# A fast block product for the last of eight projections, with its sums filled into idle time

## The chip, the cores and the metric

One NeuronCore of a Trainium2 chip runs the whole program. The metric is the device time of one execution in microseconds (us); the profiled execution is one such run taken by the hardware profiler. Engines are TensorE (PE; PEld is its weight load), VectorE (DVE), ScalarE (ACT), GpSimd (POOL) and SyncE (SP, which issues the DMAs).

## The reference

Attention with two fixed masks over 8 batches, 8 heads and 576 positions, and on its output x a gated feed-forward block:

```python
h = np.maximum(x @ w_in, 0.0)          # x: (8, 576, 512), w_in: (512, 1024)
u, v = (h[..., :d_ff // 2], h[..., d_ff // 2:])
v_n = (v - mu) / np.sqrt(var + 1e-06)  # over the last axis of v
v_s = np.einsum('ts,bsd->btd', w_spatial, v_n) + b_spatial[None, :, None]
gated = u * v_s
return (gated @ w_out).astype(np.float32)
```

The change touches u = max(x @ w_in[:, :512], 0) of batch 7 alone, and the multiply u * v_s of that batch.

## The kernel before

All products are done in fp32 precision out of two reduced-precision parts: a number is stored as a rounded part and a rest ("hi" and "lo"), and each product is three matmuls (`PROD`). So each operand of a product needs a cast (`rnd`, L492, on ACT, DVE or POOL) and a subtraction, the rest (`rest`, L506, on DVE or POOL).

The eight batches run one after the other. For each there are, in this order, the attention (scores, softmax, output x), V (`project_v`, L1092, matmuls L1072 with 512 columns), the normalisation of V (statistics L1027, a reciprocal root on POOL at L1040, the normalising step L1047), the out-projection of the batch before (`project_out`, L1446, matmuls L1465), U (`project_u`, L1111, matmuls L1132 of 128x288) and the gate, which multiplies V by `w_spatial` (`gate`, L1396, matmuls L1415) and then by U. The rows beyond position 512 are the "tail", 64 rows with their own operands (`tail`, `tail_b`) and their own matmuls (L1205, L1206).

In `project_u` each of 8 blocks of the result (two halves of positions, four row blocks) sums over 4 contraction blocks of 3 matmuls each, 96 in all, and an ACT instruction evicts it from PSUM with the ReLU (L1146).

For batches 6 and 7 (`FAST_S`) the gate is `gate_fast` (L1287), a seven-product scheme for a product of 2x2 blocks: it forms sums of the blocks of V (`total`, by `combine`, L918) and of `w_spatial`, multiplies seven pairs (`product`, matmuls L1331, phases 0 to 6 by name: a11, a12, s2, s1, s4, s3, a22), and adds the results up. Two pairs of PSUM banks, x and z, take the phases in turn: 0 into x, 1 into z, 2 onto x, 3 into z anew, 4 onto z, 5 and 6 onto x. A result that is needed twice is copied out (`keep`, L522), and a bank is added to a copy by DVE (`join`, L1363) before it is written anew. The last products are multiplied by U at L1216 (`times`).

The order of the work is not written by hand. Each operation is added with a due time (its key, from the table `KEYS`), the engines that may run it and a price for each. `Program.order` (L202) plays this forward with a list scheduler: whichever engine is free next takes the ready operation with the smallest key, unless another engine would end it earlier. The model lets DVE and POOL instructions marked with `port` exclude each other. `settle` (L364) then tries a few rearrangements of matmuls, and `emit` (L415) writes every engine's instructions in that order.

The row names below have the buffer numbers taken off: `x`, `v_raw`, `vn`, `k`, `q`, `pp` are buffers that serve several purposes over time, `m` is a PSUM bank, `g` the gated product on its way into the out-projection, `o` a copy out of PSUM, `bn` the statistics.

Of the kernel before, what the change touches and what calls it, by code (L numbers as in the profile page):

```python
# [21 lines left out]
HF = DFF // 2  # L22
# [40 lines left out]
    "tt": (6.0,),  # L63
    "tp": (-10.0, 40.0,),
# [6 lines left out]
FETCHED, FETCH_COST = 100.0, 32.0  # L71
STEP_IN, STEP_OUT = 93.0, 108.0
# [8 lines left out]
FAST_S = (6, 7)  # L81
U_IN_X = tuple(b + 1 for b in U_FIRST)
# [78 lines left out]
class Program:  # L161
# [3 lines left out]
    def __init__(self):  # L165
        self.ops, self.writer, self.readers, self.spare = [], {}, {}, {}
        self.tiled, self.port, self.kind, self.lead, self.took = {}, {}, {}, {}, {}

    def add(self, key, choices, fn, reads=(), writes=(), spare=None, tiled=0, port=(), kind=0, lead=None, took=None):
# [32 lines left out]
    def order(self):  # L202
# [22 lines left out]

        def release(n):
            for e, _ in ops[n][1]:
                heapq.heappush(wait[e], (ready_at[n][e], n))
# [7 lines left out]
        for n in range(len(ops)):  # L236
            if not left[n]:
                release(n)
        while len(issued) < len(ops):
# [75 lines left out]
    def timed(self, rows):  # L315
# [5 lines left out]
        opens = {}  # L321

        def opened(e):
# [4 lines left out]
            if any(d not in done for d in self.ops[n][3]):  # L328
                return None
            start = max([free[e], *(done[d] + LAT[on[d]][e] for d in self.ops[n][3])])  # L330
            return start, n

        while len(done) < len(self.ops):
# [28 lines left out]
        return max(*free.values(), streamed + DMA_TAIL), at  # L362

    def settle(self, issued):  # L364
# [3 lines left out]
        best, at = self.timed(rows)  # L368
        moved = True
        while moved:  # L370
# [10 lines left out]
            for (a, b), (c, d) in zip(runs, runs[1:]):  # L381
# [4 lines left out]
                for new in (  # L386
# [3 lines left out]
                    if got and got[0] < best - JOIN_GAIN:  # L390
                        best, at = got
# [46 lines left out]
def attention_moe(ctx, tc, qT, kT, ks, vl, vs, cst, w_in, w_out, wsp, wtail, out):  # L438
# [36 lines left out]
    r_vn = Ring(sb, "vn", [P, 2, NT, HF], F32R, 1)  # L475
# [482 lines left out]
    def weights():  # L958
# [3 lines left out]
        first = r_vn.new()  # L962
        for n, (key, name, i, c) in enumerate(jobs):

            def put(key=key, name=name, i=i, c=c, n=n):
                stage = (first, n) if n < NT else ((r_g if n % 2 else r_u).new(), 0)
# [120 lines left out]
    vns, tls, us, xtl, split_last = {}, {}, {}, {}, {}  # L1087
# [692 lines left out]
```

## Time and profile before

| | |
|---|---|
| median of 3 runs | 506.44 us (506.10 to 506.92) |
| profiled execution | 506.58 us, of which 504.8 us are its span |
| PE busy | 491.0 us (97% of the span) |
| DVE busy | 365.6 us (72%) |
| ACT busy | 290.3 us (58%) |
| POOL busy | 113.7 us (23%) |
| mean granted TensorE clock | 0.99 |
| chain that ended last | PE 93%, DMA 3%, DVE, POOL and ACT 1% each |

The times in the trace count from the start of the span. The part that matters lies at its end: U of batch 6 to 427.3, the gate of batch 6 from 427.3 to 442.0, V of batch 7 to 451.8, the out-projection of batch 6 to 462.9, U of batch 7 to 475.7, and the gate of batch 7 with the last out-projection to 504.8.

### The profile page before, as it was taken

Reading aid. Unit: us, or ns where it says so; the run is one execution under the profiler, and the core shown is the slowest. Engines: PE = TensorE matmul, PEld = TensorE weight load, DVE = VectorE, ACT = ScalarE, POOL = GpSimd, SP = SyncE. Lnnn points to the kernel's source line nnn. Section 1 sums busy time; section 2 is a strip of 40 time slices with the busy share of each in tenths; the row PEclk is TensorE's granted clock in tenths of the full one; section 3 lists DMA queues with packets and bytes.
Section 4 is the critical chain, followed back from the end, with each engine's and each line's share of the span. In section 5 each row is a group of like instructions: output and inputs, shape, how many; then the busy total and the mean of one; then the engine's idle time right before and its main releaser. Section 6 shows DMA issues by size and latency. Waiting matters only on the chain.

```text
span 504.8 us, 15798 instructions
## 1 busy us (share of the span) xinstructions
PE 491.0 (97%) x6374; PEld 451.3 (89%) x6374; DVE 365.6 (72%) x1114; ACT 290.3 (58%) x896; POOL 113.7 (23%) x232
## 2 busy tenths in 40 slices
PE   6599999999999999999999999999999999999997
PEld 3478898889988999899998999989999899989996
DVE  4889898987778628785389834778269796959285
ACT  5797777677546566373554764355464465435334
POOL 4554325133232013120121211121022302011000
PEclk9699999999999999999999999999999999999999
DMA  8997342432423502205224152023321051002002
GB/s 288 404 342 239 125 155 93 137 93 53 156 90 120 175 5 91 77 25 165 82 93 139 45 163 89 5 90 119 86 92 47 0 190 47 2 1 94 1 1 94
DMA packets 26968, 54.47 MB, mean 108 GB/s; under 512 B 3216, under 2 KB 11536, under 8 KB 26896
## 3 DMA queue, kind: packets, MB, share of 16 engines
q1 hardware_dynamic: 26896, 53.47, 32.0%
q8 instruction: 50, 0.82, 0.7%
q14 instruction: 22, 0.18, 0.1%
HBM read 44.02 MB, written 9.44 MB: 106 GB/s over the span
## 4 chain that ended last, share of the span: by engine, by line
PE 93%; DMA 3%; DVE 1%; POOL 1%; ACT 1%; issue 0%; SPq 0%; POOLq 0%
PE m L1132 21%; PE m L1072 20%; PE m L1465 18%; PE m L1415 15%; PE m L1331 4%; PE po L705 4%; PE po L809 3%; PE s L595 3%; PE s L738 2%; DMA q<-qT 1%; PE m L1427 1%; PE m L1428 1%; DMA k<-kT 1%; PE m L1206 0%; POOL ptl L502 0%; PE m L1205 0%
## 5 line engine op out<-in xcount | busy, mean ns | idle before, releaser
L1132 PE MATMUL m<-x,w_in_sb 128*128 128x288 f32 x768 | 105.2, 297 | 0.0
L1132 PEld LDWEIGHTS m<-x,w_in_sb 128*128 128x128 f32 x768 | 103.0, 188 | 0.6
L1072 PE MATMUL m<-w_in_sb,x 128*128 128x512 f32 (+1 forms) x408 | 99.6, 398 | 0.0
L1465 PE MATMUL m<-g,w_out 128*128 128x288 f32 x672 | 93.4, 296 | 0.2
L1465 PEld LDWEIGHTS m<-g,w_out 128*128 128x128 f32 x672 | 90.1, 188 | 2.0 <-ACT o L522 0.3
L1072 PEld LDWEIGHTS m<-w_in_sb,x 128*128 128x128 f32 (+1 forms) x408 | 74.1, 185 | 18.3
L1415 PE MATMUL m<-wsp_sb,vn 128*128 128x288 f32 x576 | 85.0, 296 | 0.0
L1415 PEld LDWEIGHTS m<-wsp_sb,vn 128*128 128x128 f32 x576 | 79.2, 189 | 0.7
L502 POOL TENSOR_SCALAR ptl<-pc 32x64 f32<-32x64 f32 (+3 forms) x98 | 38.2, 389 | 108.6 <-DVE pc L676 70.5
L652 ACT ACTIVATE pl<-pl,ml 128x64 f32<-128x64 f32 (+1 forms) x140 | 47.0, 338 | 7.8 <-DVE ml L632 7.6
L1040 POOL TENSOR_TENSOR bn<-bn,sel 128x1 f32<-128x1 f32 (+1 forms) x37 | 21.6, 586 | 131.3 <-DVE bn L1035 126.5
L510 DVE TENSOR_TENSOR g<-u,g 128x288 fp32r<-128x288 f32 x98 | 43.8, 464 | 8.6 <-POOL g L502 4.1
L500 ACT CAST g<-u 128x288 fp32r<-128x288 f32 x89 | 38.1, 435 | 19.7 <-DVE u L921 9.5
L500 ACT COPY ptl<-pc 32x320 f32<-32x320 f32 (+3 forms) x94 | 33.5, 356 | 17.2 <-DVE pc L676 15.3
L1146 ACT ACTIVATE u<-m 128x288 f32<-128x288 f32 x56 | 23.0, 410 | 35.5 <-PE m L1132 35.2
L1027 DVE BATCH_NORM_STATS2 bn<-vv 128x6 f32<-128x512 f32 (+1 forms) x29 | 19.8, 685 | 29.3 <-ACT vv L1022 29.0
L510 DVE TENSOR_TENSOR x<-po,x 128x288 fp32r<-128x288 f32 x64 | 27.4, 448 | 9.3 <-DMA v_raw<-vl 4.7
L1022 ACT ACTIVATE vv<-m 128x512 f32<-128x512 f32 (+1 forms) x29 | 17.2, 595 | 28.7 <-PE m L1072 28.4
L522 ACT CAST x<-po 128x288 fp32r<-128x288 f32 x60 | 22.2, 399 | 18.7 <-PE po L705 9.8
L632 DVE CUSTOM_DVE_ANT_0 pl<-s,cst_sb 128x64 f32<-128x64 f32 (+1 forms) x140 | 22.1, 214 | 13.0 <-PE s L595 13.0
L652 ACT ACTIVATION_READ_ACCUMULATOR pl<-pl,ml 128x1 f32 (+1 forms) x140 | 26.4, 189 | 0.0
L502 POOL TENSOR_SCALAR pts<-pc 32x288 f32<-32x288 f32 x30 | 15.7, 523 | 40.6 <-DVE pc L792 31.5
(182 smaller groups left out, 738.7 us busy)
## 6 DMA issues: line engine op xcount, KB each, us to landing
q<-qT SPq DMA_DIRECT2D x32, 295.0 KB, 4.2
v_raw<-vs SPq DMA_DIRECT2D x15, 512.0 KB, 4.1
v_raw<-vl SPq DMA_DIRECT2D x16, 384.0 KB, 4.1
k<-kT SPq DMA_DIRECT2D x16, 304.0 KB, 4.8
kbd<-ks SPq DMA_DIRECT2D x32, 144.0 KB, 5.0
outT<-o SPq DMA_DIRECT2D x32, 144.0 KB, 1.9
outT<-u SPq DMA_DIRECT2D x28, 144.0 KB, 2.1
vn<-w_in SPq DMA_DIRECT2D x4, 512.0 KB, 7.6
```

Of the source, the lines that this page charges most:

```text
L500: eng.copy(dst(), src())
L502: eng.tensor_scalar(dst(), src(), 1.0, 0.0, op0=ALU.mult, op1=ALU.add)
L510: eng.tensor_tensor(dst(), src(), f32(hi()), op=ALU.subtract)
L522: eng.copy(dst(), src())
L632: eng.tensor_tensor_reduce(out=p_sb()[:m, u, :], in0=s_ps[u % 2]()[:m, f0 : f0 + 2 * STRIDE], in1=msk[:m], scale=-SCALE, scalar=3.0e38, op ...
L652: eng.activation(p_sb()[:m, u, :], src, AF.Exp, bias=st()[:m, u : u + 1], scale=SCALE if masked else -1.0, **total,)
L1040: lambda eng: eng.tensor_tensor(bn()[:m, 9:10], bn()[:m, 8:9], sel[:m, 0:1], op=ALU.pow),
L1072: eng.matmul(v_ps()[:m, :], x_at(kt)[:, a, :], w_in_sb[:, w, kt, HF:], start=(n == 0 and i == 0), stop=(n == NT - 1 and i == 2),)
L1132: eng.matmul(u_ps()[:, :HS], w_in_sb[:, w, kt, f * P : (f + 1) * P], xs[NHP * b + kt]()[:, a, r], start=(n == 0 and i == 0), stop=(n == NT ...
L1146: lambda eng, u=u, f=f, u_ps=u_ps: eng.activation(flat(u)[:, f * HS : (f + 1) * HS], u_ps()[:, :HS], AF.Relu),
L1415: eng.matmul(s_ps()[:, :HS], vn()[:, a, kt, fs], wsp_sb[:, w, kt, r], start=(kt == 0 and i == 0), stop=False,)
L1465: eng.matmul(o_ps()[:, :HS], w_out_t[0]()[:, w, r, BLOCKS[name], j * P : (j + 1) * P], at(a), start=(first and r == 0 and i == 0), stop=(r ...
```

## The change

`project_u` hands batch 7 to a new `project_u_fast` (`FAST_U`). It is the same seven-product scheme with x as the moving and `w_in` as the stationary operand: 7 products of 2 row blocks, 2 contraction blocks and 3 matmuls, 84 in all. It needs four sums of blocks of x (`t1` to `t4`) and four of `w_in` (`s1` to `s4`), each with a cast and a rest; `one_row` adds them for each of two contraction blocks. Results are copied out by ACT without the ReLU, six joins are done by DVE, and the ReLU moves into the multiplies of batch 7's gate, which become `scalar_tensor_tensor` instructions.

The sums are added while `prog.quiet` is set. Such operations are left out when `order` plays the program forward, so the rest is ordered without them; `fill_idle` then takes them one by one and tries up to 12 gaps (`IDLE_TRIES`) of DVE or POOL that are at least 0.9 of the price long (`FIT`), keeping the place after which the modelled end is earliest.

To make room, the buffer of the normalised V is split in two (`vn0`, `vn1`), and operands of `gate_fast` that stood in x buffers move: phases 2 and 3 to `vn1`, phase 4 to `xt`. This holds for batches 6 and 7, so the gate of batch 6 is ordered anew too.

```diff
+FIT, IDLE_BIAS, IDLE_TRIES, IDLE_EPS = 0.9, 300.0, 12, 15.0
+FAST_U = (7,)
...
+        if self.quiet:
+            self.idle.append(n)
...
+    def fill_idle(self, issued):
...
+        best, at, done = self.timed(rows)
+        for n in self.idle:
+            found = []
+            for e, cost in self.ops[n][1]:
+                ready = max([done[d] + LAT[on[d]][e] for d in self.ops[n][3]], default=0.0)
+                row = rows[e]
+                for i in range(len(row) + 1):
+                    begins = at[row[i]] if i < len(row) else 1e12
+                    if begins < ready:
+                        continue
+                    since = max(ready, done[row[i - 1]] if i else 0.0)
+                    if begins - since >= FIT * cost:
+                        found.append((since + cost + (IDLE_BIAS if e == POOL else 0.0), e, i))
+            tried = []
+            for _, e, i in sorted(found)[:IDLE_TRIES]:
+                new = {**rows, e: rows[e][:i] + [n] + rows[e][i:]}
+                got = self.timed(new)
+                if got:
+                    tried.append((got[0], e, i, new, got))
+                    if got[0] <= best + IDLE_EPS:
+                        break
+            _, e, _, rows, (best, at, done) = min(tried, key=lambda x: x[0])
+            on[n] = e
...
-        issued = self.settle(issued)
+        issued = self.settle(self.fill_idle(issued))
...
-    r_vn = Ring(sb, "vn", [P, 2, NT, HF], F32R, 1)
+    r_vn = [Ring(sb, f"vn{i}_", [P, NT, HF], F32R, 1) for i in range(2)]
...
+    def project_u_fast(b, key):
...
+        prog.quiet = False
+        x, z = ([r_pm.new(held) for _ in range(2)] for _ in range(2))
...
+        product(0, "a11", "11", x)
+        keep(0, x, 0, 0)
+        product(1, "a12", "21", z)
+        join(1, z, 0, 0)
+        product(2, "s2", "t2", x, False)
+        keep(2, x, 0, 1)
+        product(3, "s1", "t1", z)
+        keep(3, z, 1, 1)
+        product(4, "s4", "22", z, False)
+        join(4, z, 0, 1)
+        product(5, "s3", "t3", x, False)
+        join(5, x, 1, 1)
+        product(6, "a22", "t4", x, False)
+        keep(6, x, 1, 0)
+
+    def one_row(key, n, r, row, rtok, values, sums, out, kept, after, engs):
...
+        cost = lambda n: [(e, {DVE: 70 + 1.04 * n, POOL: 120 + 2.3 * n}[e]) for e in engs]
+        for j in range(2):
+            hi, lo, toks = values(j)
+            add(
+                key, cost(2 * n),
+                lambda eng, j=j, hi=hi, lo=lo: eng.tensor_tensor(
+                    row[j]()[:, : 2 * n], f32(hi()), f32(lo()), op=ALU.add
+                ),
+                [*toks, *after], [rtok(j, 0), rtok(j, 1)], port=(DVE, POOL), kind=1,
+            )
+        for x, y, d, op in sums:
...
+        for name, where in out:
+            at, tok = kept[name]
+            rnd(key, n, lambda at=at: at(0, r), part(*where), [rtok(*where)], [tok(r)[0]], (ACT,))
+            rest(
+                key, n, lambda at=at: at(1, r), part(*where), lambda at=at: at(0, r),
+                [rtok(*where), tok(r)[0]], [tok(r)[1]], engs,
+            )
...
+                if b in FAST_U:
+                    add(
+                        k0 - KEYS["so"][2], [(DVE, 70 + 1.04 * HS)],
+                        lambda eng, o=o, ug=ug: eng.scalar_tensor_tensor(
+                            ug(), ug(), 0.0, o(), op0=ALU.max, op1=ALU.mult
+                        ),
+                        [(o,)], [utok], port=(DVE,),
+                    )
+                    continue
```

How the instructions stand on an engine before and after is listed below at three places around the gate of batch 6. A row is the line, the operation, output and inputs, and the shape; x2, x3 or x6 is a run of like rows. In the names, `m` is a PSUM bank, `v_raw`, `x`, `xt` and `vn__7` hold operands of the products, `kbd`, `ptl` and `pc` parts of `w_spatial` sums, `tail` and `tail_b` the operands of the tail.

PE at the start of the gate of batch 6, before, from the second product on; `kbd` with `x` is the third product, `kbd` with `v_raw` a part of the sixth, and the last two rows are the fourth:

```order
L1331 MATMUL m_6674<-wsp_sb,v_raw_6465 128x288 x6
L1331 MATMUL m_6684<-wsp_sb,v_raw_6465 128x288 x3
L1205 MATMUL m_6674<-wt_h,tail_6645 128x288
L1206 MATMUL m_6674<-wt_b,tail_b_73 128x288
L1331 MATMUL m_6684<-wsp_sb,v_raw_6465 128x288 x3
L1205 MATMUL m_6684<-wt_h,tail_6645 128x288
L1206 MATMUL m_6684<-wt_b,tail_b_73 128x288
L1331 MATMUL m_6650<-kbd_6498,x_6638 128x288 x6
L1331 MATMUL m_6662<-kbd_6498,x_6638 128x288 x6
L1331 MATMUL m_6650<-kbd_6498,v_raw_6678 128x288 x6
L1331 MATMUL m_6674<-wsp_sb,x_6643 128x288 x6
L1331 MATMUL m_6684<-wsp_sb,x_6643 128x288 x6
```

PE there after; the first two rows are the first product; L1542 is the former L1331, and L1267 and L1268 are the tail's:

```order
L1542 MATMUL m_6677<-wsp_sb,v_raw_6409 128x288 x6
L1542 MATMUL m_6689<-wsp_sb,v_raw_6409 128x288 x6
L1542 MATMUL m_6702<-wsp_sb,v_raw_6478 128x288 x6
L1542 MATMUL m_6714<-wsp_sb,v_raw_6478 128x288 x6
L1267 MATMUL m_6702<-wt_h,tail_6687 128x288
L1268 MATMUL m_6702<-wt_b,tail_b_73 128x288
L1267 MATMUL m_6714<-wt_h,tail_6687 128x288
L1268 MATMUL m_6714<-wt_b,tail_b_73 128x288
L1542 MATMUL m_6677<-kbd_6534,vn__7_6429 128x288 x6
L1542 MATMUL m_6689<-kbd_6534,vn__7_6429 128x288 x6
L1542 MATMUL m_6702<-wsp_sb,vn__7_6429 128x288 x6
L1542 MATMUL m_6714<-wsp_sb,vn__7_6429 128x288 x6
```

The six matmuls of `kbd` with `v_raw`, which stood ahead of the fourth product, now stand behind it, and the tail's matmuls follow all of the first two products.

DVE from the tail's statistics to the two joins that free the banks of the fourth product, before:

```order
L1031 BN_AGGR bn_6618<-bn_6618 128x2
L1035 TENSOR_SCALAR bn_6618<-bn_6618 128x1
L1047 TENSOR_SCALAR vv_6608<-vv_6608,bn_6618 128x512
L510 TENSOR_TENSOR x_6638<-vn_6157,x_6638 128x512
L510 TENSOR_TENSOR tail_6645<-vv_6608,tail_6645 64x512
L510 TENSOR_TENSOR tail_6655<-vv_6608,tail_6655 64x512
L510 TENSOR_TENSOR x_6643<-vv_6404,x_6643 128x512
L510 TENSOR_TENSOR x_6666<-vn_6157,x_6666 128x512
L510 TENSOR_TENSOR v_raw_6678<-vn_6157,v_raw_6678 128x512
L510 TENSOR_TENSOR v_raw_6701<-vn_6157,v_raw_6701 128x512
L1363 TENSOR_TENSOR o_6672<-m_6674,o_6672 128x288
L1363 TENSOR_TENSOR o_6688<-m_6684,o_6688 128x288
```

DVE there after (L569 is the rest, L980 a combination, L1574 the join, L1482 and L1490 the new sums):

```order
L1345 TENSOR_TENSOR pc_79<-k_6593,pc_79 96x288
L1094 TENSOR_SCALAR bn_6641<-bn_6641 128x1
L1482 TENSOR_TENSOR k_6666<-x_6311 128x576
L1106 TENSOR_SCALAR vv_6630<-vv_6630,bn_6641 128x512
L1490 TENSOR_TENSOR k_6615<-k_6666,k_6615 128x288
L569 TENSOR_TENSOR tail_6687<-vv_6630,tail_6687 64x512
L569 TENSOR_TENSOR tail_6698<-vv_6630,tail_6698 64x512
L569 TENSOR_TENSOR v_raw_6712<-vn__7_6164,v_raw_6712 128x512
L1574 TENSOR_TENSOR o_6693<-m_6702,o_6693 128x288
L569 TENSOR_TENSOR v_raw_6725<-vn__7_6164,v_raw_6725 128x512
L980 TENSOR_TENSOR u_6505<-o_6693,u_6505 128x288
L1574 TENSOR_TENSOR o_6706<-m_6714,o_6706 128x288
```

Two new sums (`k_6666`, `k_6615`) stand among the steps of the tail, and a rest and a combination now stand between the two joins.

POOL from the last cast ahead of the gate, before:

```order
L502 TENSOR_SCALAR g_1668<-u_5639 128x288
L1040 TENSOR_TENSOR bn_6618<-bn_6618,sel 128x1
L502 TENSOR_SCALAR x_6643<-vv_6404 128x512
L502 TENSOR_SCALAR tail_b_73<-vv_6608 64x512
L502 TENSOR_SCALAR tail_b_74<-vv_6608 64x512
L1040 TENSOR_TENSOR bn_6841<-bn_6841,sel 128x1
```

POOL there after:

```order
L561 TENSOR_SCALAR xt_6643<-vn__7_6164 128x512
L1099 TENSOR_TENSOR bn_6641<-bn_6641,sel 128x1
L561 TENSOR_SCALAR tail_6687<-vv_6630 64x512
L561 TENSOR_SCALAR tail_6698<-vv_6630 64x512
L1490 TENSOR_TENSOR k_6666<-k_6666,k_6615 128x288
L561 TENSOR_SCALAR tail_b_74<-vv_6630 64x512
L569 TENSOR_TENSOR x_6664<-k_6615,x_6664 128x288
L1490 TENSOR_TENSOR k_6666<-k_6666 128x288
L569 TENSOR_TENSOR x_6802<-k_6666,x_6802 128x288
```

The casts of `tail` are on POOL now, and four new sums and rests (L1490, L569) follow among and behind the casts; five more rows like these come next. Over the whole program POOL gets 15 instructions of two wide inputs, 10 of L1490, one of L1482 (512 columns) and four of L569.

## Rows read from the trace of the kernel before

**Rows 1.** The page, part 1: busy us, share of the span, instructions of each engine.

```profile
PE 491.0 (97%) x6374; PEld 451.3 (89%) x6374; DVE 365.6 (72%) x1114; ACT 290.3 (58%) x896; POOL 113.7 (23%) x232
```

**Rows 2.** The page, part 4: share of the chain that ended last, by engine.

```profile
PE 93%; DMA 3%; DVE 1%; POOL 1%; ACT 1%; issue 0%; SPq 0%; POOLq 0%
```

**Rows 3.** Windows: stretch, us, busy us (instructions) of PE, PEld, DVE, ACT, POOL; clock; DMA.

```profile
427.30:442.00 14.70, 14.70 (x108) 14.44 (x107) 13.67 (x30) 6.87 (x16) 2.04 (x3) 1.00 0.01 2
...
462.90:475.70 12.80, 12.80 (x99) 12.80 (x98) 3.78 (x7) 4.59 (x11) 0.55 (x1) 1.00 0.10 36
```

**Rows 4.** The chain in order of time: start us, us, engine, work, instructions.

```profile
442.17 9.79 PE m L1072 x42
...
463.06 12.80 PE m L1132 x96
```

**Rows 5.** DVE timeline 437 to 443: start us, us, engine, line, operation, out<-in, count.

```profile
439.40 0.82 DVE L921 TENSOR_TENSOR u<-u,u 128x288 f32<-128x288 f32 x2
440.14 0.45 DVE L1363 TENSOR_TENSOR o<-m,o 128x288 f32<-128x288 f32 x1
```

**Rows 6.** POOL by line and form: count, then busy us, mean ns, idle before.

```profile
L502 POOL TENSOR_SCALAR g<-x 128x288 fp32r<-128x288 f32 x3 | 1.3, 432 | 1.4 <-ACT pl L652 1.0 <-PE m L1465 0.4
...
L502 POOL TENSOR_SCALAR v_raw<-vn 128x512 fp32r<-128x512 f32 x2 | 1.2, 620 | 2.7 <-PE m L1331 1.8 <-PE m L1465 0.8
```

**Rows 7.** POOL timeline 424 to 437; in brackets idle before and what ended it.

```profile
425.73 0.55 POOL L1040 TENSOR_TENSOR bn<-bn,sel 128x1 f32<-128x1 f32 x1 [22.23 <-DVE bn L1035]
426.77 0.62 POOL L502 TENSOR_SCALAR x<-vv 128x512 fp32r<-128x512 f32 x1 [0.49 <-PE m L1132]
427.35 2.06 POOL L502 TENSOR_SCALAR tail_b<-vv 64x512 fp32r<-64x512 f32 x2
```

**Rows 8.** DVE timeline 424 to 437.

```profile
424.55 0.70 DVE L1027 BATCH_NORM_STATS2 bn<-vv 128x6 f32<-128x512 f32 x1 [1.95 <-ACT vv L1022]
...
426.32 0.55 DVE L1047 TENSOR_SCALAR vv<-vv,bn 128x512 f32<-128x512 f32 x1 [0.67 <-POOL bn L1040]
426.97 0.95 DVE L510 TENSOR_TENSOR x<-vn,x 128x512 fp32r<-128x512 f32 x1
427.96 2.00 DVE L510 TENSOR_TENSOR tail<-vv,tail 64x512 fp32r<-64x512 f32 x2
429.99 0.69 DVE L510 TENSOR_TENSOR x<-vv,x 128x512 fp32r<-128x512 f32 x1
...
431.20 1.29 DVE L510 TENSOR_TENSOR v_raw<-vn,v_raw 128x512 fp32r<-128x512 f32 x2
432.41 0.82 DVE L1363 TENSOR_TENSOR o<-m,o 128x288 f32<-128x288 f32 x2
...
435.58 0.46 DVE L1363 TENSOR_TENSOR o<-m,o 128x288 f32<-128x288 f32 x1 [0.66 <-PE m L1206]
```

**Rows 9.** DVE and POOL timelines 453.5 to 457.

```profile
453.67 0.17 DVE L1031 BATCH_NORM_AGGREGATE bn<-bn 128x2 f32<-128x6 f32 x1
453.78 0.46 DVE L921 TENSOR_TENSOR u<-u 128x288 f32<-128x288 f32 x1
...
455.02 0.45 DVE L510 TENSOR_TENSOR g<-u,g 128x288 fp32r<-128x288 f32 x1
...
454.82 0.69 POOL L1040 TENSOR_TENSOR bn<-bn,sel 128x1 f32<-128x1 f32 x1 [2.94 <-DVE bn L1035]
```

**Rows 10.** PE timeline 395 to 505, three rows of the gate of batch 6.

```profile
427.32 2.95 PE L1331 MATMUL m<-wsp_sb,v_raw 128*128 128x288 f32 x21
...
433.43 1.76 PE L1331 MATMUL m<-wsp_sb,x 128*128 128x288 f32 x12
...
440.95 0.94 PE L1331 MATMUL m<-ptl,v_raw 128*128 128x288 f32 x6
```

**Rows 11.** Waits of PE weight loads: what for, total us, times, longest us.

```profile
PEld m L1465 <- ACT o L522: 0.3, 1, 0.3
PEld m L1465 <- ACT u L522: 0.3, 1, 0.3
```

More of the change, by code (lines that the diff above doesn't have):

```diff
@@ L224, in begin @@
             return at
+        idle = set(self.idle)
         def release(n):
+            if n in idle:
+                for m in after[n]:
+                    for o in ENGINES:
+                        ready_at[m][o] = max(ready_at[m][o], ready_at[n][o])
+                    left[m] -= 1
+                    if not left[m]:
+                        release(m)
+                return
             for e, _ in ops[n][1]:
@@ L234, in queue @@
             )
[L236 to L239, printed above, removed]
+        for n in [n for n in range(len(ops)) if not left[n]]:
+            release(n)
+        while len(issued) < len(ops) - len(idle):
             best = None
@@ L321, in timed @@
         opens = {}
+        deps, total = self.needs(on), len(on)
         def opened(e):
@@ L327, in opened @@
             n = rows[e][heads[e]]
-            if any(d not in done for d in self.ops[n][3]):
+            if any(d not in done for d in deps[n]):
                 return None
-            start = max([free[e], *(done[d] + LAT[on[d]][e] for d in self.ops[n][3])])
+            start = max([free[e], *(done[d] + LAT[on[d]][e] for d in deps[n])])
             return start, n
-        while len(done) < len(self.ops):
+        while len(done) < total:
             best = None
@@ L361, in timed, with needs @@
             opens = {o: x for o, x in opens.items() if o != e and x}
-        return max(*free.values(), streamed + DMA_TAIL), at
+        return max(*free.values(), streamed + DMA_TAIL), at, done
+    def needs(self, on):
+        missing = set(self.idle) - set(on)
+        if not missing:
+            return {n: self.ops[n][3] for n in on}
+        found = {}
+        for n in range(len(self.ops)):
+            found[n] = set()
+            for d in self.ops[n][3]:
+                found[n] |= found[d] if d in missing else {d}
+        return {n: found[n] for n in on}
+    def fill_idle(self, issued):
+        on = {n: e for _, n, e in issued}
+        rows = {e: [n for _, n, o in issued if o == e] for e in ENGINES}
+        if not self.idle:
+            return issued
+        best, at, done = self.timed(rows)
[21 more added lines that the diff above has]
+            on[n] = e
+        return sorted((at[n], n, on[n]) for n in on)
     def settle(self, issued):
@@ L961, in weights @@
         )
-        first = r_vn.new()
+        first = [r.new() for r in r_vn]
         for n, (key, name, i, c) in enumerate(jobs):
             def put(key=key, name=name, i=i, c=c, n=n):
-                stage = (first, n) if n < NT else ((r_g if n % 2 else r_u).new(), 0)
+                stage = (first[n // 2], n % 2) if n < NT else ((r_g if n % 2 else r_u).new(), 0)
                 val, tok = in_value(c, i)
@@ L1285, in spatial_sums, with homes, home @@
         w_t["d"] = (wt_d, at_d)
+    def homes():
+        low = []
+        def home(phase):
+            if phase in (2, 3):
+                low.extend(r_vn[1].new() for _ in range(not low))
+                buf, view = low[0], lambda ap: ap[:, 2 * (phase - 2) : 2 * (phase - 1)].rearrange("p a b -> p (a b)")
+            elif phase == 4:
+                buf, view = r_xt.new(), lambda ap: ap.rearrange("p a b c -> p (a b c)")
+            else:
+                buf, view = r_v.new(), lambda ap: ap.bitcast(F32R).rearrange("p a b -> p (a b)")
+            at = lambda w: view(buf()).rearrange("p (a b c) -> p a b c", a=2, b=2)[:, w]
+            return at, lambda w: (buf, phase, w)
+        return home
```

142 lines of the change are left out of this document (117 added, 25 removed).

## The prediction, made before the changed kernel ran

> **What bounds the kernel now.** I began with the page's first part, where TensorE (PE) is busy 97% of the span [rows 1], and its fourth, where PE holds 93% of the chain that ended last [rows 2]. So a matmul less is time less, as long as PE never has to wait for what makes its operands. The windows by stage say where that condition is tight. The gate of batch 6 (427.3 to 442.0) is full on PE, and VectorE (DVE) is busy 13.67 of its 14.70 us; in U of batch 7 (462.9 to 475.7) DVE is busy 3.78 us and ScalarE (ACT) 4.59 of 12.80 [rows 3]. The granted clock is 1.00 in both, the upper of its two levels, so the clock has nothing to give or take while PE stays fed. The change takes matmuls from the second of these stages and puts its new sums mostly ahead of and into the first.
>
> **What it removes.** U of batch 7 is 96 matmuls of 128x288. As seven products, of 2 row blocks, 2 contraction blocks and 3 partial products each, it is 84. The chain gives 12.80 us for the 96, and 9.79 us for 42 of 512 columns [rows 4], thus 0.1333 and 0.2331 us for one. The twelve are worth 12 x 0.1333 = 1.60 us, and they lie on the path.
>
> **What it adds in that stage.** The eight ReLU evictions on ACT become eight copies on ACT of the same shape, and six joins of a PSUM bank with a copy come to DVE. A join of this form is the 0.45 us row at 440.14 [rows 5]: 6 x 0.45 = 2.7 us on a DVE that has 9.0 us free. Before a bank is written again PE has at least the six matmuls of its twin bank to do (0.8 us), longer than one copy or join. The ReLU goes into the gate's multiply, two inputs and 288 columns as before. Cost on the path: nothing, and if the cover failed, one join, 0.45 us.
>
> **What it adds elsewhere.** 24 sums, 16 casts and 16 rests, for batch 7's x and for the first half of w_in. The casts go to ACT, which has room in both stages [rows 3]: nothing. Of the 40 sums and rests 25 go to DVE and 15 to GpSimd (POOL) by the order listing. On DVE 288 columns with two inputs take 0.37 from start to start, as two in 0.82 us [rows 5] show. On POOL there is no wide instruction with two inputs in the trace, and this is the price in dispute. Its one-input casts take 432 ns at 288 and 620 ns at 512 columns [rows 6], hence 190 ns and 0.84 ns a column. If a second input costs a second pass, 288 columns take 190 + 2 x 0.84 x 288 = 674 ns, 256 take 620 and 512 take 1050. The lower end is the cast's own 432 ns. The upper end is the narrow two-input instruction, 0.55 us at 425.73 [rows 7], plus one pass of 0.24: 790 ns. I take 674, since it keeps the measured slope and counts both inputs; the narrow row is a power, not a sum.
>
> The Trainium skill, "GPSIMD Engine Reference", section 3.1, gives about 2.6 cycles an element for an add of two tensors on this engine, 4497 ns for 2048 columns; as an estimate from that page it is some 685 ns at 288 columns, and the sum by it would be about 0.1 us above mine. No row here shows it.
>
> **What such an instruction does to DVE.** The trace shows it in the tail of batch 6's normalisation. DVE's rest at 426.97 takes 0.95 us against 0.69 for the same shape at 429.99 [rows 8], and POOL's cast of 0.62 began at 426.77, 0.2 earlier [rows 7]. Then two casts on POOL and two rests on DVE stand crosswise: 2.06 us for two casts (0.62 alone) and 2.00 for two rests [rows 7, 8]. So a two-input DVE instruction and a wide POOL instruction wait for each other's end, and cost the sum of both. One row speaks against making this general: beside the power at 454.82, stretched to 0.69, DVE's rest at 455.02 kept its 0.45 [rows 9].
>
> The Trainium skill, "SBUF — State Buffer", section "Who interferes with whom", says that a DVE instruction with two SBUF inputs contends with a GpSimd instruction that reads SBUF, and that whoever issues first blocks the other for its whole length. By that rule all 15 POOL instructions would stop DVE where they meet; the casts agree (0.95 for 0.69 us), the power does not.
>
> **The gate of batch 6, term B.** The fourth product writes on a bank that DVE must first have joined. Before, those 12 matmuls start at 433.43 as number 46 from 427.32 [rows 10], and the joins at 432.41 take 0.82 us for two [rows 8], so the first is done by 432.86: slack 0.57. The change moves six matmuls of the sixth product behind: the fourth is now number 40, wanted at 427.32 + 40 x 0.1333 = 432.65, 0.78 earlier. That alone eats the slack. DVE's way there, from the rows of before and the order of after: statistics begin at about 424.9 (0.35 later than the row at 424.55, for one sum ahead of them that finds no gap), then 0.60 for them and 0.60 for a 512-wide rest (start to start, as two in 1.29 at 431.20 [rows 8] show), 0.11 (as 453.67 to 453.78 [rows 9]), 0.37 and 0.11 again: 426.7. There a sum of 576 columns (0.67 us by the slope of DVE's rows) starts, and POOL's power, which the tail waits for, is held by it: 427.85. The normalising step adds 0.55 and 428.4 is reached (before: 426.87 [rows 8]). The casts of the tail are now on POOL, 0.62 each: first at 429.1; the rest that follows meets the second cast, 430.45; the second rest meets POOL's new 674 ns sum and the third cast, 431.55; a rest of 0.69 meets that cast, 432.55; the join follows, done at 433.0. Against 432.65 that is 0.35. The second join then has a 512-wide rest and a 288-wide product ahead of it, which meet two more POOL instructions of 674 ns: about 434.95, against 433.0 + 6 x 0.1333 = 433.8 for PE, another 1.1. B = 1.45.
>
> **The gate's last bank, term C.** From there PE has 46 matmuls of 288 and 9 of 512 columns to the product that needs the last join: 46 x 0.1333 + 9 x 0.2331 = 8.2 us. DVE has 18 instructions of 0.37 = 6.7, a wait of 0.66 for PE's tail matmuls like that before 435.58 [rows 8], and three meetings of 0.5 (674 ns less what DVE's own order covers): 8.9. Before, that join was done at 440.59 and PE came at 440.95 [rows 5, 10], slack 0.36. C = 0.7.
>
> **Smaller terms.** A: a 256-wide weight sum on POOL (0.62) among the joins of batch 5's out-projection, covered by one DVE step of 0.37: 0.25. D: V of batch 7 waits for the multiply that frees a bank, behind three weight rests and a 512-wide POOL sum (1.05, mostly covered): 0.2. E: the last weight rests in batch 6's out-projection, 0.62 less some 0.3 of cover: 0.3. In the last out-projection the two waits of 0.3 us [rows 11] stay as they are.
>
> **Sum.** -1.60 + 0.25 + 1.45 + 0.7 + 0.2 + 0.3 = +1.30. The profiled execution took 506.58 us, 504.8 of span and 1.78 around it; it stands 0.14 above the median of 506.44. So 507.88 in its terms, 507.74 in those of the median: 507.75.
>
> **The rivals.**
> Cheap sums: POOL's two-input instruction costs what its cast does. Some 7.5 meetings on the path are then 0.24 us shorter, 1.8 in all, and 1.1 of waiting is left: 506.44 - 1.60 + 1.1 = 505.95, no change that can be told. For it: only the cast rows. Against it: a second input has to be read.
> Whole gain: the sums don't hold DVE, like the power at 454.82, or what they hold is covered. The waits go to nothing and 506.44 - 1.60 = 504.84. For it: the power rows and the free time of DVE outside the gate; it decides where the meetings add under 0.6 us. Against it: the gate is short on DVE with no POOL sum at all, and the fourth product is 0.78 us earlier.
> Dearer sums: at 790 ns all 15 are 0.117 dearer, and if all are felt that is 1.75: 509.5. For it: the narrow row's 0.55.
> That the change does not do what it says: the sums could come late for U itself. The last ones stand among the out-projection of batch 6, at the latest two products ahead of use, so I give it nothing apart.
>
> **How the numbers follow.** My forecast 0.44 (its own range 507.45 to 508.3), dearer sums 0.12, cheap sums 0.23, whole gain 0.21. A measurement of this kernel tells about 0.2% (1.0 us) from no change. Faster is the whole gain alone, 0.21; within 0.2% are the cheap sums, 0.23; slower are the forecast and the dearer sums, 0.56. The range goes from the whole gain to the dearer sums, 504.8 to 509.5, with some 0.06 left out below (a loss covered and a little more saved) and 0.1 above.
>
> **What would show it.** Right: U of batch 7 as 84 matmuls in 11.2 us; POOL rows of 288 columns and two inputs near 0.67; PE idle before the fourth product of gate 6 (0.3 to 0.4 and about 1.1 us, released by DVE's joins) and before its last product; DVE rests of 1.0 to 1.3 us beside POOL sums. Wrong: POOL sums under 0.5 us, DVE rests of unchanged length beside them, or no idle PE between 427 and 442. If PE waits inside U of batch 7, the cover there was misjudged.

## The result and the profile after

The changed kernel takes 508.87 us (median of 7 runs, 508.06 to 510.38), the kernel before 506.26 us (7 runs beside it, 505.37 to 507.08). The ratio is 1.0053, 95% interval 1.0036 to 1.0069: slower by 2.6 us, where the prediction said slower by 1.3.

Part 1 and part 4 of the page of the kernel after, against [rows 1, 2]:

```profile
PE 492.3 (97%) x6362; PEld 449.9 (89%) x6362; DVE 381.9 (75%) x1145; ACT 294.2 (58%) x910; POOL 133.1 (26%) x249
...
PE 85%; DVE 10%; POOL 2%; issue 2%; ACT 1%; POOLq 0%; DVEq 0%
```

Twelve matmuls have gone, and yet the span is 2.2 us longer. PE's share of the chain fell from 93% to 85%, and DVE has 10% of it where it had 1%. DVE's 31 instructions more brought 16.3 us of busy time, 0.53 each. Seven of them are sums of 512 or 576 columns, which take 0.68 to 0.76 us by themselves; the narrow ones take 0.42 to 0.46. So only a part of the excess over 0.45 is stretching, and the single rows below have to show it.

The early stages of the program differ between executions by up to two microseconds: in the twelve traces V of batch 6 starts between 385.84 and 387.80. So all traces are compared from the start of V of batch 6, ahead of all that the experiments touch, to the end of the span. These are that row of the kernel before and that of the kernel after (PE timeline):

```profile
386.89 11.37 PE L1072 MATMUL m<-w_in_sb,x 128*128 128x512 f32 x48
```

```profile
386.40 11.37 PE L1131 MATMUL m<-w_in_sb,x 128*128 128x512 f32 x48
```

That is 504.8 - 386.89 = 117.91 us before and 507.0 - 386.40 = 120.60 us after, +2.69. This figure is called the stretch below. It comes from one trace of each kernel. The differences of the medians lie within 0.5 us of it; for e6 the medians differ by 0.8 us more.

PE's timeline of after through the gate of batch 6, V of batch 7 and the out-projection of batch 6, with PE's idle time and its releaser in brackets (against [rows 10]):

```profile
427.12 3.34 PE L1542 MATMUL m<-wsp_sb,v_raw 128*128 128x288 f32 x24
...
432.55 1.06 PE L1542 MATMUL m<-wsp_sb,vn__7_6429 128*128 128x288 f32 x6
434.54 1.07 PE L1542 MATMUL m<-wsp_sb,vn__7_6429 128*128 128x288 f32 x6 [0.93 <-DVE o L1574]
...
444.15 1.06 PE L1542 MATMUL m<-ptl,v_raw 128*128 128x288 f32 x6 [0.74 <-DVE o L1574]
...
448.46 6.57 PE L1131 MATMUL m<-w_in_sb,x 128*128 128x512 f32 x27 [0.20 <-DVE u L1281]
...
460.90 5.71 PE L1686 MATMUL m<-g,w_out 128*128 128x288 f32 x41 [0.23 <-DVE g L569]
```

The second half of the fourth product starts at 434.54 behind a wait of 0.93 us for a join, the last bank's product at 444.15 behind 0.74 for another, and two waits of 0.2 follow. Before, the PE timeline has none from V of batch 6 to the last matmul. These rows count a wait only from the end of the matmul before it; the weight loads ahead of the matmuls show more of it (what for, total us, times, longest us):

```profile
PEld m L1542 <- DVE o L1574: 2.7, 4, 1.2
...
PEld m L1686 <- DVE g L569: 0.7, 2, 0.5
PEld m L1131 <- DVE u L1281: 0.6, 1, 0.6
...
PEld m L1433 <- DVE o L1711: 0.2, 1, 0.2
```

2.7 + 0.7 + 0.6 + 0.2 = 4.2 us, and 4.2 - 1.6 is 2.6 of the 2.69. By stage (the columns of [rows 3]: PE, PEld, DVE, ACT, POOL, clock, DMA):

```profile
427.10:441.15 14.05, 13.12 (x95) 12.36 (x93) 11.73 (x22) 7.38 (x19) 10.49 (x12) 1.00 0.01 2
441.15:454.87 13.72, 12.79 (x58) 9.94 (x57) 12.61 (x31) 3.66 (x8) 3.81 (x4) 1.00 0.00 1
454.87:466.46 11.59, 11.37 (x85) 11.13 (x84) 11.26 (x25) 7.87 (x21) 6.44 (x9) 1.00 0.15 53
466.46:478.90 12.44, 12.44 (x94) 12.21 (x93) 8.55 (x18) 5.15 (x13) 0.62 (x1) 1.00 0.14 49
```

In the second of these stretches DVE is busy 12.61 of 13.72 us; in the kernel before it had 5 of 9.8 us free after the gate. POOL is busy 10.49 us in the first, against 2.04 in a gate of like length before. The clock is 1.00 in all of them, as before.

DVE's free time is used up even ahead of the gate. These are the windows of U of batch 6, before and then after:

```profile
411.70:427.30 15.60, 15.60 (x110) 15.06 (x109) 11.22 (x29) 9.30 (x25) 1.08 (x2) 1.00 0.39 119
```

```profile
411.50:427.10 15.60, 15.60 (x110) 15.05 (x109) 15.57 (x36) 9.21 (x25) 2.03 (x3) 1.00 0.37 117
```

Before, 4.4 us of DVE were free there. After, it is busy 15.57 of 15.60 us, and so comes to the tail's steps with no time in hand.

### The profile page after: what moved, and what is told of

Read it like the earlier page. It is cut to its first block, busy times and chain, and to the rows that moved or that the text cites. A ratio compares the mean times of both kernels' runs of the same rounds, so it can differ in the third digit from the quotient of the medians.

```text
span 507.0 us, 15841 instructions
## 1 busy us (share of the span) xinstructions
PE 492.3 (97%) x6362; PEld 449.9 (89%) x6362; DVE 381.9 (75%) x1145; ACT 294.2 (58%) x910; POOL 133.1 (26%) x249
## 4 chain that ended last, share of the span: by engine, by line
PE 85%; DVE 10%; POOL 2%; issue 2%; ACT 1%; POOLq 0%; DVEq 0%
PE m L1131 18%; PE m L1686 16%; PE m L1194 15%; PE m L1636 15%; PE po L764 3%; PE po L868 3%; PE m L1542 3%; PE s L654 3%; PE m L1433 2%; PE s L797 2%; PE m L1648 1%; PE m L1649 1%; PE s L1918 1%; DVE u L980 1%; POOL ptl L561 1%
## 5 line engine op out<-in xcount | busy, mean ns | idle before, releaser
L1194 PE MATMUL m<-x,w_in_sb 128*128 128x288 f32 x672 | 92.2, 297 | 0.0
L1194 PEld LDWEIGHTS m<-x,w_in_sb 128*128 128x128 f32 x672 | 90.2, 188 | 0.6
L569 DVE TENSOR_TENSOR g<-u,g 128x288 fp32r<-128x288 f32 x98 | 45.2, 479 | 8.6 <-POOL g L561 4.6
L1099 POOL TENSOR_TENSOR bn<-bn,sel 128x1 f32<-128x1 f32 (+1 forms) x37 | 23.6, 641 | 95.0 <-DVE bn L1094 90.2
L1208 ACT ACTIVATE u<-m 128x288 f32<-128x288 f32 x48 | 19.7, 410 | 28.3 <-PE m L1194 27.1
L569 DVE TENSOR_TENSOR x<-po,x 128x288 fp32r<-128x288 f32 x64 | 27.3, 446 | 7.9 <-DMA v_raw<-vl 4.7
L581 ACT COPY u<-m 128x288 f32<-128x288 f32 x36 | 14.2, 399 | 14.4 <-PE m L1686 6.7
L559 ACT COPY pts<-pc 32x288 f32<-32x288 f32 x34 | 14.8, 434 | 11.6 <-DVE pc L851 10.8
```

Of the source, the lines that this page charges most:

```text
L559: eng.copy(dst(), src())
L569: eng.tensor_tensor(dst(), src(), f32(hi()), op=ALU.subtract)
L581: eng.copy(dst(), src())
L1099: lambda eng: eng.tensor_tensor(bn()[:m, 9:10], bn()[:m, 8:9], sel[:m, 0:1], op=ALU.pow),
L1194: eng.matmul(u_ps()[:, :HS], w_in_sb[:, w, kt, f * P : (f + 1) * P], xs[NHP * b + kt]()[:, a, r], start=(n == 0 and i == 0), stop=(n == NT ...
```

## The experiments

All are compared with runs of the kernel before on the same chip. Of the theories, A says that POOL's 15 sums, at some 0.8 us, are the cost; B that it is the new order (places of the gate's operands, the fourth product 0.78 us earlier); C that DVE is short whoever makes the sums; D that DVE and POOL are one resource for two-input work; E that the sums merely stand in the wrong place; F that they fit, but place and engine decide.

| run | ratio (95%) | stretch against before, us |
|---|---|---|
| the changed kernel | 1.0053 (1.0036 to 1.0069) | +2.69 |
| e1, places only, U as before | 1.0006 (0.9994 to 1.0018) | +0.27 |
| e2, no sums | 0.9979 (0.9967 to 0.9991) | -1.31 |
| e3, POOL reads one input | 0.9995 (0.9983 to 1.0007) | -0.51 |
| e4, all sums on DVE | 1.0047 (1.0031 to 1.0063) | +2.94 |
| e5, PE takes other work in its wait | 1.0049 (1.0030 to 1.0067) | +2.75 |
| e6, no sums in the gate | 1.0089 (1.0068 to 1.0109) | +3.85 |
| e7, DVE's sums read one input | 1.0021 (1.0007 to 1.0035) | +0.93 |
| e8, sums of w_in only | 0.9991 (0.9977 to 1.0005) | -0.69 |
| e10, sums of x only | 1.0009 (0.9994 to 1.0024) | +0.17 |
| e9, any gap allowed | 0.9997 (0.9982 to 1.0012) | -0.18 |

**e1, places only.**

```diff
-FAST_U = (7,)
+FAST_U = ()
```

> The changed kernel with batch 7's U made as before (96 matmuls); the split of the buffer of V and the new places of the gate's operands stay. Theory A (the sums on POOL, at about 0.8 us for 288 columns and two inputs, hold DVE in the gate of batch 6): no sums, so no loss, ratio to before 1.000 within 0.002, about 506.3 us. Theory B (the new places and the order that follows from them cost it, since the fourth product comes 0.78 us earlier): ratio 1.003 or more, 507.5 us or more, with PE idle between 427 and 444.

Measured 506.71 against 506.33 us: no change that can be told. Of the stretch 0.27 us remains, and the interval ends at 1.0018, under B's 1.003. Theory B is out as the cause of 2.6.

**e2, no sums.**

```diff
+        for name, raw in (("t1", "11"), ("t2", "21"), ("t3", "22"), ("t4", "11")):
+            moving[name] = moving[raw]
+        for name, raw in (("s1", "a11"), ("s2", "a12"), ("s3", "a22"), ("s4", "s3")):
+            still[name] = plain[raw]
-        prog.quiet = True
-        for r in range(2):
-            bufs = [(r_q if r else r_k).new() for _ in range(2)]
-            one_row(
...
-        prog.quiet = False
```

> The changed kernel without the 40 sums and rests and 16 casts: the seven products of U take blocks of x and of w_in as they are, so that part of the computation is left out. Theories A and C (DVE is short in the gate whoever makes the sums): the whole worth of twelve matmuls, 1.60 us less than before, 504.7 us, ratio 0.997. Theory B: the loss in the gate stays, 506 us or more.

505.33 against 506.33 us, and the stretch is 1.31 us shorter: against e1, which has the same places, 1.58 (1.38 by the medians). The twelve matmuls are worth what 12 x 0.1333 says, and no cost of the copies, joins and the ReLU in the multiply can be seen. So the sums, with their casts and rests, cost all of the loss: the changed kernel's +2.69 less -1.31, 4.0 us, near the 4.2 that the weight loads showed.

**e3, POOL reads one input.** The order on every engine is that of the changed kernel. The rests on POOL are changed in the same way as the sums shown here.

```diff
+    def plain_sum(eng, dst, x, y, op):
+        if eng is nc.gpsimd:
+            eng.tensor_scalar(dst, x, 1.0, 0.0, op0=ALU.mult, op1=ALU.add)
+        else:
+            eng.tensor_tensor(dst, x, y, op=op)
```

> The changed kernel in the same order on every engine, but each of the 15 new sums and rests on POOL reads one of its two inputs (the other is left out, so part of the sums is missing): 432 ns instead of about 800 at 288 columns. Theory A: about 1.1 us of waiting is left of some 4.2, so 505.8 us, ratio 0.999. Theory C: DVE's own 25 instructions are the cost, so it stays at 508 us or more, ratio above 1.003.

505.94 against 506.33 us. With the cast's price on POOL the 4.0 us of waiting are 0.8 (-0.51 less -1.31), though all 25 instructions on DVE and all 16 casts on ACT are there. This run is the prediction's rival of cheap sums (505.95 us), made real. It speaks for A and against C.

**e4, all sums on DVE.** A second change, not shown here, lets a sum that fits into no gap be placed anywhere late in the program.

```diff
-                (("t1", (0, 0)), ("t3", (0, 1)), ("t2", (1, 1)), ("t4", (1, 0))), moving, [], (DVE, POOL),
+                (("t1", (0, 0)), ("t3", (0, 1)), ("t2", (1, 1)), ("t4", (1, 0))), moving, [], (DVE,),
...
-                (("s2", (0, 0)), ("s1", (1, 1)), ("s4", (1, 0)), ("s3", (0, 1))), still, [], (DVE, POOL),
+                (("s2", (0, 0)), ("s1", (1, 1)), ("s4", (1, 0)), ("s3", (0, 1))), still, [], (DVE,),
```

> The changed kernel with all 40 sums and rests on DVE and none on POOL (a sum that fits into no gap goes to the place where the planned end is earliest). Theory A: no sum holds DVE, and the time is below before, 505 to 506 us, ratio 0.998. Theory C: 15 instructions of 0.37 to 0.6 us more, some 6 us, on an engine with 1.0 us free in that gate: 508 us or more, ratio 1.003 to 1.006.

508.83 against 506.33 us, and A is out in its turn: with no sum on POOL the loss is about the same. It only stands elsewhere. PE's waits of e4 (PE timeline):

```profile
430.60 0.40 PE L1274 MATMUL m<-wt_h,tail 128*128 128x288 f32 x1 [0.65 <-DVE tail L576]
...
467.01 1.07 PE L1440 MATMUL m<-x,w_in_sb 128*128 128x288 f32 x6 [0.74 <-DVE o L1718]
...
469.83 3.25 PE L1440 MATMUL m<-x,vn__8_6793 128*128 128x288 f32 x21 [1.36 <-ACT vn__8_6793 L566]
```

0.65 us in the gate, and 2.1 us inside U of batch 7, for a join and for operands that come too late. So POOL's share is not the cause by itself: in the places that this plan found for it, the work that e3 made cheap on POOL costs as much when DVE does it. Whether other places on DVE would cost less is not shown. That is theory D, formed from e3 and e4.

**e5, PE takes other work in its wait.** After `settle`, the six matmuls of `kbd` with `v_raw` are put ahead of the fourth product's second half.

```diff
+        row = [n for n in rows[PE] if n not in self.early]
+        first = min(row.index(n) for n in self.late)
+        rows = {**rows, PE: row[:first] + self.early + row[first:]}
```

> The changed kernel with the six matmuls of kbd with v_raw moved on PE ahead of the second half of the fourth product, where PE waited 0.93 us; DVE and POOL keep their order. Theory D (DVE and POOL together are one engine for two-input work, and their row through the gate of batch 6 is the bound): the wait of 0.93 gets small and the one before the last bank (0.74) grows by about as much; time as the changed kernel, 508.9 us, ratio to before 1.005. Theory B (PE's order, with the fourth product 0.78 us earlier, costs it): 0.8 us less, 508.1 us, ratio 1.0035.

509.02 against 506.39 us: as slow as the changed kernel. The interval (1.0030 to 1.0067) holds D's ratio of 1.005 and B's of 1.0035, so the time alone does not decide; the stretch, +2.75 for +2.69, and the waits do. PE's waits of e5 in the gate:

```profile
435.38 1.07 PE L1547 MATMUL m<-wsp_sb,xt 128*128 128x288 f32 x6 [0.31 <-ACT o L586]
...
439.47 1.06 PE L1547 MATMUL m<-ptl,v_raw 128*128 128x288 f32 x6 [0.36 <-DVE o L1583]
...
443.65 1.06 PE L1547 MATMUL m<-ptl,v_raw 128*128 128x288 f32 x6 [0.76 <-DVE o L1583]
```

The wait of 0.93 is gone; 0.31 and 0.36 have come in between, and the last one of 0.76 stays. It was not the wait that I had expected to grow, but the loss is the same: PE came sooner to its next bank and stood there. The weight loads of the gate wait 2.9 us in all, against 2.7 in the changed kernel. This change of PE's order gained nothing while DVE's row behind it had the same length.

**e6, no sums in the gate.** What fits nowhere is placed as in e4; this second part of the edit is not shown.

```diff
-                    if begins < ready:
+                    if begins < ready or 430000.0 < begins < 450000.0:
```

> The changed kernel, but no sum may go into a gap that begins in the 20 us around the gate of batch 6 and the first part of V of batch 7; what fits nowhere goes to the place with the earliest planned end. Theory E (the sums merely stand in the wrong place): no wait in the gate and the gain of 1.60 us kept for the most part, 505 to 506 us, ratio below 0.999. Theory D (17 us of two-input work have no room ahead of U of batch 7, wherever they stand): PE waits inside U of batch 7 instead, for 4 us or more; 509 us or more, ratio 1.005 to 1.010.

511.07 against 506.39 us, worse than the changed kernel by the medians (its profiled execution, 509.71, was the fastest of six, so its stretch is likely too small). The gate has no wait now; PE's waits of e6 are in the out-projection of batch 6 (L1693) and in U of batch 7 (L1440):

```profile
458.12 1.07 PE L1693 MATMUL m<-g,w_out 128*128 128x288 f32 x6 [0.86 <-DVE g L576]
459.59 3.64 PE L1693 MATMUL m<-g,w_out 128*128 128x288 f32 x24 [0.39 <-DVE g L576]
463.51 1.83 PE L1693 MATMUL m<-g,w_out 128*128 128x288 f32 x11 [0.28 <-DVE g L576]
...
471.37 2.79 PE L1440 MATMUL m<-x,vn__8_6860 128*128 128x288 f32 x19 [1.32 <-DVE vn__8_6860 L576]
```

1.5 and 1.3 us of them in view (D had asked for all inside U). E is out in the form tried here: pushed out of the gate, the sums come too late, or stand between DVE's steps of the out-projection. So keeping sums out of the gate is not enough; that other places could do better, e9 shows.

**e7, DVE's sums read one input.** The edit is that of e3 for the other engine:

```diff
+    def plain_sum(eng, dst, x, y, op):
+        if eng is nc.vector:
+            eng.tensor_scalar(dst, x, 1.0, 0.0, op0=ALU.mult, op1=ALU.add)
```

> The changed kernel in the same order, but the new sums and rests on DVE read one of their inputs (the other is left out, so part of the sums is missing), and so are shorter and outside the meetings; the 15 on POOL keep both. Theory A (POOL's 15 alone, at 0.8 us, are the cost): near the changed kernel, 508 us or more, ratio 1.003 or more. Theory D (both shares add up on one resource): about half of the waits are left, 507.2 us, ratio 1.002.

507.77 against 506.39 us. Of 4.0 us of waiting 2.2 are left. The interval (1.0007 to 1.0035) still holds A's 1.003; against A stands the stretch, +0.93 for +2.69. Against what I had expected, the shortened instructions were not all outside the meetings: one of them took 1.04 us for 0.30, at 447.00, while POOL's sum of 512 columns ran from 445.06 for 2.81 us (1.41 in the changed kernel). e3 took 3.2 us away by making POOL's 15 instructions cheaper, e7 1.8 by making DVE's 25 cheaper; together that is 5.0, more than there was (4.2 for 3.6 by the medians). So the two shares do not each have a cost of their own. That what costs is what lies above the free time fits this, but is an inference.

**e8 and e10, half of the sums.** In e8 the first call of `one_row` goes, and the products take unsummed blocks of x:

```diff
+        for name, raw in (("t1", "11"), ("t2", "21"), ("t3", "22"), ("t4", "11")):
+            moving[name] = moving[raw]
```

> The changed kernel with the sums of w_in alone; the products take blocks of x as they are, so the sums of x are left out, half of the new work. If each sum costs the same, half of some 4.3 us of waiting is left: 1.60 gained, 2.15 lost, 506.9 us, ratio 1.001. Theory D (what fits into the free time of DVE is free, and only the excess costs): under 1 us of waiting, 505.6 us, ratio 0.9985.

In e10 the second call goes, and they take unsummed blocks of `w_in`:

```diff
+        for name, raw in (("s1", "a11"), ("s2", "a12"), ("s3", "a22"), ("s4", "s3")):
+            still[name] = plain[raw]
```

> The changed kernel with the sums of x alone; the products take blocks of w_in as they are, so the sums of w_in are left out, the other half of the new work. If the halves' waits simply add up, 4.3 less the 0.9 to 1.1 us that the half with w_in left, 3.3, are here: 508.1 us, ratio 1.003. Theory D (only the excess over the free time costs, so the two halves together cost more than apart): 2 us of waiting or less, 506.7 us or less, ratio below 1.001.

e8 took 505.77 against 506.39 us, e10 506.68 against 506.49. By the stretch e8 leaves 0.6 us of waiting, e10 1.5. Together that is 2.1, and both halves at once cost 4.0. So the halves cost more together than apart, as when each alone finds most of the free time. The gaps were filled anew in both runs: e8 has 5 instructions on POOL where the changed kernel has 8 for this half, e10 has 7 as there. A part of e8's small loss may come from that.

**e9, any gap allowed.** The same work as the changed kernel, and one line, which changes four settings of the second pass:

```diff
-FIT, IDLE_BIAS, IDLE_TRIES, IDLE_EPS = 0.9, 300.0, 12, 15.0
+FIT, IDLE_BIAS, IDLE_TRIES, IDLE_EPS = 0.0, 0.0, 60, 0.0
```

> The changed kernel with the same work, but each sum tries every gap among 60, however short, with no handicap for POOL, and takes the one with the earliest planned end; 8 of the 40 sums and rests come to POOL instead of 15. Theory D in its strict form (17 us of two-input work don't fit ahead of their use, wherever they stand): near the changed kernel, 508 us or more, ratio 1.004. Theory F (the work fits, but each instruction on POOL takes the 0.8 us from DVE that 0.37 us of DVE would have cost, and where it stands decides): most of the waits go, 506.0 to 506.8 us, ratio 1.000 within 0.0015.

506.27 against 506.49 us: no difference to the kernel before that can be told, and 2.9 us of stretch less than the changed kernel. PE's one wait in the gate is now this one:

```profile
434.43 1.06 PE L1542 MATMUL m<-wsp_sb,vn__7_6430 128*128 128x288 f32 x6 [0.27 <-DVE o L1574]
```

So D in its strict form falls: the work does fit, all but about 1.1 us of it (-0.18 less -1.31). In the changed kernel the second pass looked only at gaps of at least 0.9 of the price, and took the first of up to twelve that cost the planned end at most 15 ns, or else the cheapest of them. A gap that is too short by the plan may cost less than one that is long enough but stands ahead of a join; this is argued, not shown. With 8 POOL instructions for 15 there are also fewer meetings; e9 changes both, and how much is due to which was not taken apart. None of the kernels that do the whole work beats the kernel before.

## Why the prediction was right, and where its size was off

**The gain of 1.60 us** stands. U of batch 7 in the chain of after:

```profile
466.62 2.40 PE m L1433 x18
469.02 7.44 PE m L1433 x54
...
477.52 1.61 PE m L1433 x12
```

18 + 54 + 12 matmuls in 2.40 + 7.44 + 1.61 = 11.45 us, against 11.2 forecast; 0.2 of it is a wait inside U for a join of the out-projection, a cover that the prediction had misjudged. e2 against e1 gives 1.58 us.

**The meetings** are of the kind that was forecast. DVE's timeline of after on the way to the two joins (L1574), against [rows 8]:

```profile
424.65 0.68 DVE L1086 BATCH_NORM_STATS2 bn<-vv 128x6 f32<-128x512 f32 x1
...
426.39 0.76 DVE L1482 TENSOR_TENSOR k<-x 128x576 f32<-128x576 f32 x1
427.59 0.55 DVE L1106 TENSOR_SCALAR vv<-vv,bn 128x512 f32<-128x512 f32 x1 [0.45 <-POOL bn L1099]
...
429.01 0.68 DVE L569 TENSOR_TENSOR tail<-vv,tail 64x512 fp32r<-64x512 f32 x1 [0.51 <-POOL tail L561]
430.21 0.69 DVE L569 TENSOR_TENSOR tail<-vv,tail 64x512 fp32r<-64x512 f32 x1 [0.52 <-POOL tail L561]
430.93 1.19 DVE L569 TENSOR_TENSOR v_raw<-vn__7_6164,v_raw 128x512 fp32r<-128x512 f32 x1
432.05 0.44 DVE L1574 TENSOR_TENSOR o<-m,o 128x288 f32<-128x288 f32 x1
432.41 0.73 DVE L569 TENSOR_TENSOR v_raw<-vn__7_6164,v_raw 128x512 fp32r<-128x512 f32 x1
433.06 1.05 DVE L980 TENSOR_TENSOR u<-o,u 128x288 f32<-128x288 f32 x1
434.04 0.44 DVE L1574 TENSOR_TENSOR o<-m,o 128x288 f32<-128x288 f32 x1
```

and POOL's:

```profile
426.50 1.06 POOL L1099 TENSOR_TENSOR bn<-bn,sel 128x1 f32<-128x1 f32 x1 [2.05 <-DVE bn L1094]
428.23 1.95 POOL L561 TENSOR_SCALAR tail<-vv 64x512 fp32r<-64x512 f32 x2 [0.67 <-DVE vv L1106]
430.26 1.31 POOL L1490 TENSOR_TENSOR k<-k,k 128x288 f32<-128x288 f32 x1
431.66 0.94 POOL L561 TENSOR_SCALAR tail_b<-vv 64x512 fp32r<-64x512 f32 x1
432.69 1.11 POOL L569 TENSOR_TENSOR x<-k,x 128x288 fp32r<-128x288 f32 x1
433.76 1.01 POOL L1490 TENSOR_TENSOR k<-k 128x288 f32<-128x288 f32 x1
437.17 0.80 POOL L569 TENSOR_TENSOR x<-k,x 128x288 fp32r<-128x288 f32 x1 [2.40 <-ACT x L559]
```

The forecast's points on this way and what came: statistics at 424.9 (424.65); POOL's power held by the 576-wide sum until 427.85 (426.50 + 1.06 = 427.56); second rest of the tail done at 431.55 (430.90); first join done at 433.0 (432.49); second at 434.95 (434.48). DVE's rest at 430.93 took 1.19 us beside a POOL sum of 1.31, and its product at 433.06 took 1.05 for 0.45. Two things came otherwise. DVE's rests of the tail kept 0.68 and 0.69 us; it was POOL's sum at 430.26 that was held (1.31). And the first half of the fourth product started at 432.55, 0.1 us late instead of 0.35, so nearly all of B stands before the second half.

**Term by term.** A, the out-projection of batch 5: 66 matmuls took 8.99 us before and 9.25 after, +0.26 (forecast 0.25). B: 434.54 instead of 427.12 + 46 x 0.1333 = 433.25, +1.29 (1.45). C: from there 46 x 0.1333 + 9 x 0.2331 = 8.23 us would be 442.77, and PE got there at 444.15: +1.38, forecast 0.7. D: V's remaining 8 x 0.1333 + 39 x 0.2331 = 10.16 us took 444.15 to 454.87, +0.56, forecast 0.2. E: 84 x 0.1333 = 11.20 took 11.59, +0.39 (0.3). U itself +0.25 (0). Together 4.13 for 2.90.

A hit its size by another way than the one named. POOL's weight sum at 398.99 stretched one of DVE's rests from 0.45 to 0.62 us; the larger part of the delay, 0.33, is a 256-wide sum on DVE itself, at 398.49, ahead of the statistics that POOL's power waits for. That A agrees is in part luck.

**What was mis-sized** is the price of POOL's instruction with two inputs, and with it terms C and D. I took 674 ns at 288 columns. The one at 437.17, which DVE did not hold, took 0.80 us, the other end of my range (790 ns); e9, where fewer meet, shows the same (mean ns behind the first figure):

```profile
L1490 POOL TENSOR_TENSOR k<-k,k 128x288 f32<-128x288 f32 x1 | 1.3, 1312 | 0.1
...
L569 POOL TENSOR_TENSOR x<-k,x 128x288 fp32r<-128x288 f32 x1 | 0.8, 811 | 3.8 <-issue 3.8
...
L569 POOL TENSOR_TENSOR vn__8_6778<-pp,vn__8_6778 128x256 fp32r<-128x256 f32 x1 | 0.7, 734 | 0.0
```

0.81 at 288 columns and 0.73 at 256 where POOL was not held, 1.31 where it was. The slope of the casts, counted twice, was too low a guide; the power's 0.55 with one pass on it was nearer, and so was the price in the change's own plan, 120 + 2.3 x 288 = 782 ns. The measured 508.87 us lies between my 507.75 and the rival of dearer sums, 509.5. e3 gives a size for it: 0.37 us less on each took 3.2 us away, so 0.13 us more would be some 1.1 us if it went in proportion, which is an estimate. The terms came out 1.23 above the forecast.

In D the price is plain: V's wait of batch 7 stands behind a rest that POOL's sum of 512 columns held, and that sum took 1.41 us where I had 1.05.

```profile
444.87 1.41 POOL L1482 TENSOR_TENSOR pp<-w_in_sb 128x512 f32<-128x512 f32 x1 [2.94 <-DVE w_in_sb L569]
```

```profile
445.06 1.51 DVE L569 TENSOR_TENSOR vn__8_6781<-pp,vn__8_6781 128x256 fp32r<-128x256 f32 x1
```

In C, which grew most, by 0.68 us, dearer meetings are about half. Five wide POOL instructions follow each other there, from 437.17 to 441.94. From start to start the two full meetings, at 440.22 and 441.20 on DVE, took 0.98 us each for 0.37, so 0.61 and not my 0.5. With 0.43 for the one at 438.32 and some 0.2 of smaller ones the meetings come to 1.8 us for my 1.5. Another 0.25 are two pauses of 0.12 where an instruction reads what the one just before it made (437.28 to 437.77, 437.77 to 438.32), which 18 x 0.37 left out; the kernel before has such pauses too (0.49 from a join at 435.58 to the product at 436.07).

**What was right by half only**: that the fourth product's earlier place "alone eats the slack". e5 shows that moving PE's work there does not change the time, and e1 that without sums the new order costs no more than can be told (0.27 us of stretch). The waits stand at the joins because DVE is late there, not because PE is early.

The Trainium skill's figure ("GPSIMD Engine Reference", section 3.1; some 685 ns by my estimate) was below the trace as well; the measurement decides, 0.80 us. The rule that the prediction took from the Trainium skill, "SBUF — State Buffer", section "Who interferes with whom", agrees with the rows of wide sums shown here: one side is held in each meeting (1.19 us for 0.69 on DVE at 430.93, 1.31 for 0.80 on POOL at 430.26).

## What to carry to other kernels

When two engines exclude each other, idle time of one is not room of its own: price a piece of work there by what it takes from the other where the two meet, here up to 0.6 us of DVE's time for a sum that DVE does in 0.37. Work that is put into gaps of a plan should be judged by the end of the chain that follows it, not by the length of the gap: e9, with the same work in other gaps and seven instructions fewer on POOL, left 1.1 us of waiting instead of 4.0. Moving the waiting engine's work about did not help (e5), since the row of the engine that it waits for stayed as long.

## What the runs showed of the hardware

A DVE instruction with one wide input in SBUF can be held as well: in the changed kernel the normalising step (`TENSOR_SCALAR`, 512 columns) took 0.96 us beside a POOL sum that had begun 0.07 us earlier, against 0.55 at 427.59. e5, e6 and e7 show it too (0.96, 0.95 and 0.96 us). The Trainium skill ("SBUF — State Buffer", section "Who interferes with whom") names `tensor_scalar` among the instructions that can take the shared pair of ports, where its operands allow; the prediction had counted two-input instructions alone. The step lies on the way to term E, whose wait ends at 460.90. The two rows:

```profile
458.98 0.96 DVE L1106 TENSOR_SCALAR vn__8_6900<-vn__8_6900,bn 128x512 f32<-128x512 f32 x1
...
458.91 0.74 POOL L1490 TENSOR_TENSOR pp<-pp,pp 128x256 f32<-128x256 f32 x1
```

A join, which reads one of its two inputs from a PSUM bank, was not held: at 434.04 it kept 0.44 us while POOL's sum of 1.01 us, begun at 433.76, ran beside it.
